# Queries in 512-byte rows with interleaved positions, loads by need, and a first block in two parts

## The chip, the cores and the metric

The kernel runs on one core of a Trainium2 chip. The metric is the device time of one execution in microseconds (us). A kernel's time is the median of its runs. A profile is taken of one of these runs, and its span is about 2 us shorter than the run's time (323.6 against 325.27 us for the kernel before).

The engines are PE (matrix products), DVE, ACT and POOL (elementwise work), and SP, whose queue issues nearly all loads and stores here. "SPq" and "ACTq" in a trace are the queues of SP and ACT when they issue a DMA. Where one of them waits, what stands behind it in the same queue waits too: in the changed kernel an activation on ACT starts at 73.45 us, 0.05 us after a transpose that ACT had been issuing since 71.93 left its queue.

## The reference

```
scores = q k^T / sqrt(64);  ret = scores * gamma_h^(i-j) for i >= j, else 0      # 8 batches, 8 heads, 576 tokens
x      = (ret v), heads side by side                                             # 4608 x 512
h      = x @ w_in;   g = h * sigmoid(beta * h);   out = g @ w_out                # 512 -> 2048 -> 512, float32 out
```

## The kernel before

Attention goes by tiles of 128 tokens. A tile needs its queries, keys and values scaled and cast to bf16, its queries and keys transposed, masked scores, values, a state product, and a cross product with the state of the earlier tiles. Its result is copied from PSUM into `xT`, the transposed input of the second part. That part goes by blocks of 512 tokens: "up" (x by w_in, then an activation on ACT into `gT`), then "down" (gT by w_out, copied to `ot` and stored). Block 8 is the "tail block": the last 64 tokens of each of the eight batches.

The order of the program is laid by hand. A list `fill` holds the steps of up and down. Streams of attention steps, each with a position, are merged into it. The parts that matter are these, with cuts marked `...`:

```python
def load(i):                                  # one tile: three loads of 256 KB, rows of 64 floats = 256 bytes
    t = stage.tile([P, 3, H, D], F32, name="qkvn", tag="qkvn", bufs=NQ)
    for j, src in enumerate((q, k, v)):
        ...
        nc.sync.dma_start(t[:, j], src[b, :, c * P:(c + 1) * P, :].rearrange("h s d -> s h d"))

def a_X(i):                                   # later tiles: transposed by a DMA that ACT issues
    nc.scalar.dma_start_transpose(qkT..., L["qk"]...)

def a_O(i):
    ...
    (nc.scalar.copy if i < CB else nc.vector.tensor_copy)(xT[:, :, x0:x0 + P], O[:])    # dense, bf16

def down(m, ms, f0, fn=4, n0=0, nn=d_model):
    ...
    nc.vector.tensor_copy(ot, po[:, :nn])
    if m < B:                                 # a batch's block: 128 rows in one store
        nc.sync.dma_start(out[r0:r0 + P, n0:n0 + nn], ot)
    else:                                     # the tail block, which comes last: two stores of 64 rows
        for x in range(2):
            nc.sync.dma_start(out[r0:r0 + TL, n0:n0 + nn], ot[x * TL:(x + 1) * TL])

for i in range(CB):                           # the first four tiles, with a filler matmul ahead of each
    warm_up(1, 256)
    a_sc(i); a_st(i); a_cross(i, True)
    ...                                       # cast of tile i + 1, or of weights
    a_O(i)
    ...                                       # transposes of tile i + 1
```

## Time and profile before

| | before |
|---|---|
| time, median of 3 | 324.23 us (323.68 to 324.70) |
| span of the profiled run | 323.6 us |
| first up matmul of block 0 | 20.71 us |
| first down of block 0 | 35.94 us |
| first up of block 1 | 56.62 us |
| first down of block 1 | 80.73 us |
| start of the last copy to `ot` | 318.09 us |
| from there to the end | 5.5 us |

The five points in time are the milestones. Each is read off PE's timeline (the first matmul of that kind), and the last one off DVE's. The prediction shows the stretches between them.

One more view of the kernel before is needed later: the copies into `xT`. The columns are the count, then the shortest, median and longest duration in ns, then when the first and last ran.

```profile
L280 DVE CAST xT<-O x32: 673/680/692, 50.0 to 262.8; 128x512 bf16<-128x512 f32 x32
L280 ACT CAST xT<-O x3: 586/586/586, 9.0 to 16.2; 128x512 bf16<-128x512 f32 x3
```

Every copy of one form takes the same time, 0.68 us on DVE and 0.59 us on ACT.

### The profile page before, as it was taken

Reading aid. Unit: us, or ns where it says so; the run is one execution under the profiler, and the core shown is the slowest. Engines: PE = TensorE matmul, PEld = TensorE weight load, DVE = VectorE, ACT = ScalarE, POOL = GpSimd, SP = SyncE. Lnnn points to the kernel's source line nnn. Section 1 sums busy time; section 2 is a strip of 40 time slices with the busy share of each in tenths; the row PEclk is TensorE's granted clock in tenths of the full one; section 3 lists DMA queues with packets and bytes.
Section 4 is the critical chain, followed back from the end, with each engine's and each line's share of the span. In section 5 each row is a group of like instructions: output and inputs, shape, how many; then the busy total and the mean of one; then the engine's idle time right before and its main releaser. Section 6 shows DMA issues by size and latency. Waiting matters only on the chain.

```text
span 323.6 us, 5348 instructions
## 1 busy us (share of the span) xinstructions
PE 303.9 (94%) x2122; PEld 156.0 (48%) x2157; DVE 114.3 (35%) x201; ACT 133.0 (41%) x242; POOL 105.2 (33%) x126
## 2 busy tenths in 40 slices
PE   7879987987999999999999999999999999999993
PEld 3543444865444544444444554444444544444452
DVE  6545666444243344323432353233323430020021
ACT  4547402675115721672047215730473047207500
POOL 4643773823556344431433336332430000000000
PEclk9999999999999999999999999999999999999999
DMA  9999999989999999999999999943213110011022
GB/s 169 218 361 388 353 197 218 198 217 184 188 235 218 186 249 191 217 249 169 242 240 209 182 226 193 207 94 98 67 39 61 65 67 0 32 65 35 0 65 67
DMA packets 152458, 53.85 MB, mean 166 GB/s; under 512 B 142944, under 2 KB 144368, under 8 KB 152432
## 3 DMA queue, kind: packets, MB, share of 16 engines
q1 hardware_dynamic: 122832, 46.15, 68.0%
q10 hardware_dynamic: 29600, 7.35, 15.9%
q8 instruction: 17, 0.28, 0.4%
q14 instruction: 9, 0.07, 0.1%
HBM read 36.71 MB, written 9.44 MB: 143 GB/s over the span
## 4 chain that ended last, share of the span: by engine, by line
PE 66%; DMA 15%; SPq 14%; issue 1%; POOL 1%; ACT 1%; DVE 1%; ACTq 0%; POOLq 0%
PE po L322 31%; PE ph L309 26%; SPq L84 13%; DMA qkvn<-in_v_dram 5%; DMA wt<-in_moe_w_in_dram 4%; DMA qkT<-qk 3%; PE O L270 2%; PE sc L237 2%; PE O L256 2%; DMA qkvn<-in_k_dram 2%; PE st L292 1%; SPq L148 1%; DVE w_in_sb L156 0%; ACTq L214 0%; SPq L81 0%
## 5 line engine op out<-in xcount | busy, mean ns | idle before, releaser
L309 PE MATMUL ph<-xT,w_in_sb 128*128 128x512 bf16 (+1 forms) x625 | 128.9, 357 | 4.1 <-POOL w_in_sb L156 1.3
L322 PE MATMUL po<-w_out_sb,gT 128*128 128x512 bf16 (+2 forms) x588 | 126.5, 367 | 1.9 <-ACT gT L311 0.9
L311 ACT ACTIVATE gT<-ph,beta_sb 128x512 bf16<-128x512 f32 (+1 forms) x160 | 100.3, 645 | 59.5 <-PE ph L309 53.4
L309 PEld LDWEIGHTS <-w_in_sb 128*128 128x128 bf16 x640 | 61.1, 98 | 63.5 <-POOL w_in_sb L156 1.9
L322 PEld LDWEIGHTS <-gT 128*128 128x128 bf16 x608 | 57.5, 98 | 63.7 <-issue 1.0
L242 DVE TENSOR_TENSOR R<-sc,causal 128x512 bf16<-128x512 f32 x72 | 46.3, 685 | 70.1 <-PE sc L237 70.1
L329 DVE COPY ot<-po 128x512 f32<-128x512 f32 (+2 forms) x38 | 25.1, 662 | 112.8 <-PE po L322 96.2
L202 POOL TENSOR_TENSOR qk<-qkvn,gq 128x512 bf16<-128x512 f32 x35 | 36.5, 1044 | 86.0 <-issue 29.4
L204 POOL TENSOR_TENSOR vn<-qkvn,gv 128x512 bf16<-128x512 f32 x36 | 37.8, 1049 | 27.2 <-DMA qkvn<-in_v_dram 14.0
L297 ACT CAST sbd<-st 64x256 bf16<-64x256 f32 x48 | 17.6, 366 | 59.3 <-PE st L292 48.7
L297 ACT CAST end<-st 64x256 bf16<-64x256 f32 x16 | 5.9, 367 | 42.2 <-PE st L292 40.8
L280 DVE CAST xT<-O 128x512 bf16<-128x512 f32 x32 | 21.8, 681 | 0.8 <-PE O L270 0.5
L203 POOL CAST qk<-qkvn 128x512 bf16<-128x512 f32 x28 | 17.4, 621 | 6.4 <-DMA qkvn<-in_k_dram 6.0
L270 PE MATMUL O<-R,vn 128*64 128x128 bf16 x288 | 16.2, 225 | 0.1
L237 PE MATMUL sc<-qkT 64*128 64x128 bf16 x288 | 14.3, 218 | 1.6 <-DMA qkT<-qk 0.8
L237 PEld LDWEIGHTS <-qkT 64*128 64x128 bf16 x288 | 8.2, 94 | 15.7 <-issue 11.7
L292 PE MATMUL st<-vn,qk 128*128 128x128 bf16 x128 | 12.4, 219 | 2.2 <-POOL vn L204 2.2
L270 PEld LDWEIGHTS <-vn 128*64 128x64 bf16 x288 | 10.0, 109 | 4.5 <-issue 0.7
L292 PEld LDWEIGHTS <-qk 128*128 128x128 bf16 x128 | 8.6, 97 | 3.6 <-issue 2.1
L168 POOL TENSOR_SCALAR w_out_sb<-wt,rbeta_sb 128x512 bf16<-128x512 f32 x4 | 8.5, 2113 | 3.7 <-DMA wt<-in_moe_w_out_dram 3.7
L256 PE MATMUL O<-qkT,sbd 128*128 128x128 bf16 x96 | 9.5, 221 | 0.0
L226 PE MATMUL T<-ident,qk 128*128 128x128 bf16 x64 | 6.0, 221 | 2.7 <-DVE xT L280 1.3
(46 smaller groups left out, 64.3 us busy)
## 6 DMA issues: line engine op xcount, KB each, us to landing
qkvn<-in_q_dram SPq DMA_DIRECT2D x32, 256.0 KB, 5.1
qkvn<-in_k_dram SPq DMA_DIRECT2D x32, 256.0 KB, 5.1
qkvn<-in_v_dram SPq DMA_DIRECT2D x32, 256.0 KB, 5.4
out_dram<-ot SPq DMA_DIRECT2D x32, 256.0 KB, 3.4
wt<-in_moe_w_out_dram SPq DMA_DIRECT2D x4, 1024.0 KB, 9.3
wt<-in_moe_w_in_dram SPq DMA_DIRECT2D x3, 1024.0 KB, 11.2
wt<-in_moe_w_in_dram SPq DMA_DIRECT2D x2, 512.0 KB, 6.9
qkvn<-in_q_dram SPq DMA_DIRECT2D x8, 128.0 KB, 4.8
```

The source lines that it names most:

```text
L84: nc.sync.dma_start(t[:, j], src[b, :, c * P:(c + 1) * P, :].rearrange("h s d -> s h d"))
L202: (nc.vector if i == 0 else nc.gpsimd).tensor_tensor(qk[:, 0], t[:, 0], gq_b, ALU.mult)
L204: nc.gpsimd.tensor_tensor(vn[:], t[:, 2], gv_b, ALU.mult)
L237: nc.tensor.matmul(sc[j][:, p, :], L["kT"][r, p, :], L["qT"][r, p, :], start=True, stop=True, skip_group_check=True)
L242: nc.vector.tensor_tensor(R[:, j], sc[j][:], m_b, ALU.mult)
L270: nc.tensor.matmul(O[j * D:(j + 1) * D, p, :], vn[:, 2 * p + j, :], R[:, j, p, :], start=p == 0 and not (early and crossed), stop=early or ...
L292: nc.tensor.matmul(st[:, p, :], heads(L["qk"][:, 1], p), heads(L["vn"], p), start=(c == 0 and p == 0), stop=True, skip_group_check=True)
L297: nc.scalar.copy(s[r, :, j * D:(j + 1) * D], st[r, :, j * D:(j + 1) * D])
L309: nc.tensor.matmul(ph[:, :tn], w_in_sb[:, ko, fo * P:(fo + 1) * P], xT[:, ko, x0:x0 + tn], start=(ko == 0), stop=(ko == KO - 1))
L311: nc.scalar.activation(gT[:, fo, t0:t0 + tn], ph[:, :tn], ACT.Silu, scale=beta_sb[:, fo:fo + 1])
L322: nc.tensor.matmul(po[:, :nn], gT[:, fo, ms * P:(ms + 1) * P], w_out_sb[:, fo, n0:n0 + nn], start=(fo == 0), stop=(fo == FO - 1))
L329: nc.vector.tensor_copy(ot, po[:, :nn])
```

## The change

The intent is to relieve the DMA at the start. A batch's queries come as rows in which four neighbouring positions lie side by side, so two loads with rows of 512 bytes stand where four loads read twice as many rows of 256 bytes. A partition then holds tokens 4p to 4p+3. Keys and values stay as they were, so the scores of a tile come out with interleaved columns: the mask is built for that order, and the copy into `xT` puts the columns back, with a step of four elements. Loads go out at chosen steps of the program. Block 0 starts when three of its four tiles are done, with parts of 384 and 128 tokens. The fillers between the first tiles are dropped. The tail block moves ahead of the last batch's block.

The diff, cut to its core:

```diff
+    blocks = list(range(B - 1)) + [B, B - 1]          # tail block before the last batch's
...
+    def load_q(b):
+        t = stage.tile([P, H, CB, D], F32, name="qn", tag="qn", bufs=2)
+        r = q[b, :, :MB, :].rearrange("h (p i) d -> p h (i d)", i=CB)
+        for u in range(2):
+            w = slice(u * CB * D // 2, (u + 1) * CB * D // 2)
+            nc.sync.dma_start(t.rearrange("p h i d -> p h (i d)")[:, :, w], r[:, :, w])
...
-    nc.gpsimd.affine_select(out=causal[:], in_=causal[:], pattern=[[1, P]], ...
+    nc.gpsimd.affine_select(out=causal[:], in_=causal[:], pattern=[[1, CB], [CB, PC]], ...
...
+        x = xt(B if b is None else b)[:, :, c * P:(c + 1) * P]
+        if b is not None:
+            x = x.rearrange("k p (s i) -> k p i s", i=CB)
+            O = O.rearrange("k p (i s) -> k p i s", i=CB)
-            (nc.scalar.copy if i < CB else nc.vector.tensor_copy)(xT[:, :, x0:x0 + P], O[:])
+            (nc.scalar.copy if i < CB else nc.vector.tensor_copy)(x, O[:])
...
-    for i in range(CB):
-        warm_up(1, 256)
+    for i in range(CB - 1):
         a_sc(i)
         a_st(i)
...
-    fill = [F(up, 0, fo) for fo in range(FO)]
+    fill = [F(up, 0, fo, 0, part) for fo in range(4)] + [F(up, 0, fo, part, MB - part) for fo in range(4)]
+    fill += [F(up, 0, fo) for fo in range(4, FO)]
...
+               [(12.2, F(load_q, 1))] + [(12.2, F(load_kv, n)) for n in range(CB, E)],
...
-            st += [(at, F(a_sc, i)), (at + 3, F(load, i + NQ))]
+                    st += [(at - 31, F(load_q, b)), (at - 19, F(pre_q, b, 0)), (at - 17, F(pre_q, b, 1)),
+                           (at - 13.5, F(x_q, b, 0)), (at - 12, F(x_q, b, 1))]
+                    st += [(at - 28, F(load_kv, n)), (at - 27.5, F(load_kv, n + 1)), (at - 15, F(pre, i)),
+                           (at - 14.5, F(pre, i + 1)), (at - 10.5, F(x_k, b, c // 2))]
```

## The prediction

> **What bounds the kernel now.** I read the page's busy shares first, then the table of stretches, then the start on PE, then the chain that ended last and the tail. The page:
>
> ```profile
> span 323.6 us, 5348 instructions
> PE 303.9 (94%) x2122; PEld 156.0 (48%) x2157; DVE 114.3 (35%) x201; ACT 133.0 (41%) x242; POOL 105.2 (33%) x126
> PEclk9999999999999999999999999999999999999999
> ```
>
> PE is busy for nearly the whole span at full clock; no other engine passes 41%. The stretches show where it is not (columns: stretch, length, then busy time of PE, PEld, DVE, ACT, POOL, clock, DMA share, GB/s):
>
> ```profile
> 0.00:20.70 20.70, 15.38 (x137) 8.86 (x137) 12.49 (x35) 10.52 (x22) 9.91 (x22) 1.00 1.15 226
> 20.70:35.94 15.24, 14.32 (x62) 6.16 (x65) 7.90 (x17) 10.29 (x15) 7.29 (x11) 1.00 1.05 387
> 44.00:56.62 12.62, 10.44 (x90) 5.65 (x93) 7.99 (x15) 2.64 (x6) 5.91 (x6) 1.00 1.36 222
> 56.62:80.73 24.11, 21.07 (x245) 16.88 (x244) 10.82 (x18) 15.68 (x39) 12.11 (x14) 1.00 1.08 199
> 80.73:318.40 237.67, 235.56 (x1557) 115.42 (x1587) 69.66 (x111) 93.14 (x160) 63.20 (x73) 1.00 0.76 141
> ```
>
> From 80.73 to 318.4 PE lacks 2 us of 238. Work there can be moved, not shortened: 25 matmuls of 512 columns take 5.39 us in the chain, 0.216 each, and one attention tile about 1.2 us (scores 0.33, values 0.34, state 0.22, cross 0.33). Time can be won in the first 80.73 us and in the last 5. In the first 20.7 PE holds only four tiles (5 us) and fillers; its waits:
>
> ```profile
> 18.48 0.38 PE L292 MATMUL st<-vn,qk 128*128 128x128 bf16 x4 [0.47 <-POOL vn L204]
> 20.71 0.39 PE L309 MATMUL ph<-xT,w_in_sb 128*128 128x512 bf16 x1 [0.95 <-POOL w_in_sb L156]
> ```
>
> A tile every 3.6 us: that is its three 256 KB loads at 218 GB/s, so the start is DMA-bound. And at the end of block 1 the chain runs over a late load, a POOL cast, a transpose issued by ACT, and only then the activation that PE wants:
>
> ```profile
> 71.86 6.25 DMA qkvn<-in_k_dram
> 78.16 0.62 POOL qk L203
> 78.80 1.35 ACTq L214
> 80.20 0.48 ACT gT L311
> 80.73 0.38 PE po L322
> ```
>
> ACT stands 3.2 us there. In block 1 it is full: 32 half activations of 0.44 (14.2), four state copies of 0.75 (3.0), two transposed-tile copies of 0.58 and four transpose issues of 1.25 to 1.87 (6.1) make 24.5, against a stretch of 24.1.
>
> **What the Trainium skill says.** (1) "DMA: Bandwidth & Descriptors", Specifications: line rate needs transfers of at least 512 B. The trace agrees for 256 B: 218 GB/s between 4 and 16 us (256-byte rows), 387 between 24 and 38 us (2 KB rows); 512-byte loads are not in it. (2) "SBUF — State Buffer", The DMA port swizzle: consecutive accesses inside a 16-byte line run at full rate. The new moving operand of scores and cross is runs of 32 bf16, 64 B, so I count no slowdown; the copies into xT now write every fourth bf16, 8 bytes apart, and this trace has nothing like it. (3) "TensorE: Matmul & The Clock Gate", What's actually happening: idle PE falls to half clock. The change drops the fillers between the first tiles; the clock was 1.00 in every stretch before, so this is a risk and no expectation.
>
> **The change, part by part.**
>
> *Queries in 512-byte rows.* A batch's 1 MB takes 4.8 us at 218 GB/s. At 387 it would take 2.7; halfway (a fixed cost per row, fitted to 256 B at 218 and 2 KB at 387, my estimate) 3.6. Gain 1.2 to 2.1 us of DMA per batch. After 80.73 it is hidden, PE being dense.
>
> *The start.* Loads begin to flow at about 3.0 (first landing 4.2 less 1.2). After: query halves land near 4.7 and 6.2, the first keys 7.4, then 1.2 each: values of tile 2 at 13.3. So DMA leaves the path, and a chain of engines takes its place, since keys are now transposed tile by tile behind the mask: key cast 0.43, transposes 0.35, copy 0.42, scores 0.40, mask 1.29, with 0.1 of signalling at each step: 3.4 per tile. The first has more ahead of it (POOL's query product ends 7.8, transposes 8.6, DVE's copy of twice the size 0.8, key transpose and copy): scores at about 10 in place of 6.8. Mask 0 ends 11.7, mask 1 15.1, mask 2 18.4; values and split copy follow, so block 0 begins at 19.7 in place of 20.71. This order leaves tile 3 (1.6 us with transposes) inside block 0.
>
> *Block 0 up.* Eight matmuls of 384 columns (1.3), key transpose and copy of tile 3 with a stall of 0.6, eight more (1.3), tile 3 to 24.8, its copy 0.6, sixteen of 128 columns (0.9) to 26.4. The third weight piece, which lands near 23 (before: 24.4), is ready. Then 48 matmuls, 10.4: up ends at 36.8 against 35.94. So here the change is 0.9 behind.
>
> *Block 0 down, tiles 4 and 5.* Before, 35.94 to 56.62: 20.7 us with over 3 us of idle PE, because tile 4's loads waited for w_out and POOL for its casts. After: the last w_out piece lands near 39 (before 40.76), is cast by 41.5, batch 1's queries land at 42 to 43, tile 4 by 45, tile 5 by 47.5. PE reaches the query transposes at 45.4, so it meets no wait. 16 steps of 0.863 (13.8), tile 4 (0.9), tile 5 (1.2), transposes (about 1.5), a mask wait 0.5 and the copy into xT at the end 0.8: 18.9. Block 1 starts at 55.7 against 56.62, 0.9 ahead.
>
> *Block 1 up.* ACT: 16 half activations (7.1) and 8 full (5.5), state copies of tiles 6 and 7 (1.5), four transpose issues (5 to 6.5), no transposed-tile copies: 19.1 to 20.6, plus about 1.9 of waits for tile 7 before the second half. Down of block 1 starts near 77.3. Before it started at 80.73 with tiles 8 and 9 and tile 10's scores done (2.45 of PE work), after with tile 8's scores only (0.33). Gain: 80.73 - 77.3 - 2.1 = 1.3, and about 0.3 more because loads now go out at fixed steps and not when a stage buffer comes free: 1.6.
>
> *From there.* The same matmuls, tiles and 28 DMA transposes; PE stays dense, so the lead of 1.6 is carried.
>
> *The tail.* The tail block now goes before the last batch's block, so the last rows leave with one transfer per piece in place of two:
>
> ```profile
> 318.09 0.29 DVE ot L329
> ```
> ```profile
> 320.06 1.19 SPq L336 DMA_DIRECT2D out_dram<-ot  x2
> ```
>
> Six issues of 0.6 queue behind each other until 321.25, though the last copy is done at 318.38. With three, each of the first two is issued before the next copy ends, and the last starts at 318.4 and ends at 319.0: gain 2.2.
>
> Sum: 1.6 + 2.2 = 3.8, so 324.2 - 3.8 = 320.4. I take 320.2.
>
> **The rivals.**
> 1. *The early loads win more.* If the start is worth what the DMA saves and the engine chain is shorter than I sum it (transposes and masks overlapping), block 0 begins at 17 to 18 and the lead grows to 4 or 5: 316 to 317. For: PE has over 20 us of slack before 80.73, and the author lays parts of 384 and 128 tokens for just this. Against: DVE must do cast, copy and mask in series for each tile.
> 2. *ACT as the bound.* ACT works in order, and a transpose that is not ready blocks the activations behind it, as at 78.80. In block 1 four transposes fall within some 11 steps, and the third and fourth wait for POOL, which has four query products of 1.04 and 1.65 for each tile in front. If the fourth waits 2 us, the gain of block 1 is gone and only the tail is left: 322.
> 3. *Strided access costs.* If a strided xT copy takes twice 0.68, up to 0.6 is added at each of four early copies on the path; if the 64-byte runs slow scores and cross by a quarter, 56 groups of 0.33 add 4.6. Together 323 to 327. Against: the 16-byte rule.
> 4. *DMA hidden anyway.* True from 80.73 on; the 10 us or so of DMA saved later are worth nothing.
>
> **Range and chances.** The tail is the surest term (1 to 2.5). The first 80 us may give -1.5 to +5. Hence 316.5 to 323.3. Over 2% faster needs less than 317.9, a gain of 6.3, which takes rival 1 nearly in full: 0.20. Slower by 2% needs rival 3 in full: 0.02. Within 2%: 0.78.
>
> **What would show it.** Step by step in the changed profile: 512-byte query loads at 290 to 390 GB/s in the first microseconds; first 384-column matmul at 19 to 20.5, with the mask chain ahead of it and no DMA; up of block 0 ending at 36 to 37.5; first half-width matmul of block 1 at 55 to 56.5; ACT full, not PE, until down of block 1 starts at 76 to 78.5; dense PE after it with scores still 0.33 for eight; three output issues after the last block's pieces and some 3 us from the last matmul to the end in place of 5.5. The prediction is wrong if the first block starts before 18 or after 21.5, if PE shows idle time after block 1, if the clock drops under 1.00 in the first block, or if scores or xT copies take longer than before.

## The result, and the profile after

The changed kernel takes **328.92 us** (median of 4 runs, 327.39 to 329.30) against 324.27 us for the kernel before on the same chip. The ratio is 1.0136, with a 95% interval of 1.0099 to 1.0173. Ratios here are the mean time of one kernel's fast runs over that of the other's fast runs of the same rounds, so they are not quite the ratio of the medians. Executions over 1.5% slower than the fastest of the same kernel are left out of the means. The result counts as the same at 2%, but the interval lies above 1, and the time is outside the predicted range.

One warning on the profiles: the profiled run of the kernel before was its slowest (325.27 us), and that of the changed kernel its fastest (327.39 us). The two spans therefore differ by 1.6 us where the medians differ by 4.65. Two more profiles of the unchanged changed kernel, taken later, are nearer the typical run, and so is the profile of an experiment (e4) that differs from the kernel before in the tail alone. Times are in us from the start of the span:

| | before | e4: before, new tail | after | after again (e13) |
|---|---|---|---|---|
| up of block 0 starts | 20.71 | 20.67 | 21.38 | 21.25 |
| down of block 0 starts | 35.94 | 35.91 | 41.12 | 41.63 |
| up of block 1 starts | 56.62 | 56.78 | 61.44 | 61.68 |
| down of block 1 starts | 80.73 | 80.28 | 83.17 | 84.88 |
| last copy starts | 318.09 | 317.36 | 322.48 | 324.53 |
| span | 323.6 | 320.2 | 325.2 | 327.2 |

The row of block 1's down needs a correction. The kernel before enters it with 2.45 us of attention on PE done (tiles 8 and 9 and the scores of 10), the changed one with 0.33 us. So 83.17 is really a lag of 83.17 - 80.73 + 2.12 = 4.6 us, and the last copy, 322.48 - 318.09 = 4.4 us late, agrees. The story is then short: 5.2 us are lost by the end of block 0's up, they are not won back in block 1, they are carried through the dense middle, and the tail returns 2.8.

The page of the changed kernel:

```profile
span 325.2 us, 5293 instructions
...
PE 306.7 (94%) x2137; PEld 156.5 (48%) x2137; DVE 132.9 (41%) x207; ACT 133.3 (41%) x232; POOL 101.7 (31%) x127
...
PEclk9559999999999999999999999999999999999999
```

DVE gained 18.6 us of work, and the second and third of the 40 slices show half clock, of which neither the clock row nor any duration of the kernel before shows a trace. The stretches between the milestones (columns as in the prediction: stretch, length, busy time of PE, PEld, DVE, ACT, POOL, clock, DMA share, GB/s):

```profile
0.00:21.38 21.38, 13.61 (x106) 9.04 (x107) 13.02 (x35) 8.91 (x16) 11.51 (x30) 0.69 1.09 246
21.38:41.12 19.74, 17.38 (x108) 8.99 (x108) 12.29 (x27) 13.70 (x23) 9.46 (x7) 0.90 1.04 365
41.12:61.44 20.32, 18.18 (x134) 9.56 (x133) 12.04 (x20) 3.19 (x7) 12.88 (x13) 1.00 1.09 244
61.44:83.17 21.73, 18.26 (x160) 11.95 (x160) 7.58 (x12) 12.89 (x27) 8.61 (x10) 1.00 0.98 214
83.17:322.50 239.33, 239.27 (x1633) 116.91 (x1631) 87.68 (x116) 94.61 (x162) 59.24 (x68) 1.00 0.65 132
```

The last line is as predicted: PE lacks 0.06 us of 239, so a lag at 83 us is a lag at the end. The second line is where most was lost: block 0's up takes 19.7 us in place of 15.2. PE's timeline shows how (start, length, instruction, count, and in brackets the idle time before it with what ended it):

```profile
14.37 0.61 PE L302 MATMUL sc<-qT,kT 64*128 64x128 bf16 x8
...
21.38 2.85 PE L381 MATMUL ph<-xT,w_in_sb 128*128 128x384 bf16 x8 [0.83 <-DVE rbeta_sb L443]
...
29.67 11.62 PE L381 MATMUL ph<-xT,w_in_sb 128*128 128x128 bf16 x64 [1.83 <-ACT xT L353]
```

Eight small matmuls take 0.61 where 0.40 is normal, and the first eight matmuls of 384 columns take 2.85; a few us later the same eight take 1.47. That is half clock. The last line is a wait of 1.83 us for ACT's copy of tile 3 into `xT`. The copies themselves:

```profile
L353 DVE CAST xT<-O x32: 679/1291/1310, 57.2 to 264.6; 128x512 bf16<-128x512 f32 x32
L353 ACT CAST xT<-O x3: 1301/1302/1307, 14.5 to 28.3; 128x512 bf16<-128x512 f32 x3
```

The median copy went from 0.68 to 1.29 us on DVE and from 0.59 to 1.30 on ACT. The shortest, 679 ns, are the tail's tiles, which are still written densely.

In block 1 the profile's chain of what released what, which in the kernel before went over one late load, goes over two here. This is its last part:

```profile
65.61 5.50 DMA qn<-in_q_dram
71.11 0.07 issue
71.18 2.05 POOL qs L234 x2
73.23 0.17 ACTq L262
73.45 0.48 ACT gT L383
73.97 0.61 PE ph L381 x4
```

Read from the bottom: PE waits for an activation, ACT's activation stands behind a transpose that ACT issues (L262), and the transpose waits for POOL's query products and these for a load of queries. The upper half must not be taken at its word. Releasers are inferred, and the load at 65.61 holds the queries of batch 3, whose products come after the transposes of batch 2 in the program. Batch 2's queries were issued at 49.24 and scaled at once. Then ACT's queue, with the two transposes of batch 2's queries and an activation between the second and the next one:

```profile
49.24 2.24 SPq L81 DMA_DIRECT2D qn<-in_q_dram  x2
...
55.47 4.04 POOL L234 TENSOR_TENSOR qs<-qn,gq 128x512 bf16<-128x512 f32 x4 [1.40 <-DMA qn<-in_q_dram]
...
70.47 1.33 ACTq L262 DMA_TRANSPOSE qT<-qs  x1
...
71.93 1.47 ACTq L262 DMA_TRANSPOSE qT<-qs  x1
73.45 0.47 ACT L383 ACTIVATE gT<-ph,beta_sb 128x256 bf16<-128x256 f32 x1 [1.12 <-POOL qs L234]
```

The query products were done at 59.5, 11 us before the first of these transposes. The key transposes follow at 73.58 and 78.70, with their casts done by 62.4 and 68.7, 11 and 10 us before. So batch 2's data were there. What PE waits for, 2.1 us in all, are activations that stand behind the transposes in ACT's queue, 1.25 to 1.47 us at each. I took this at first for late loads, held up by stores that wait in SP's queue for DVE. Such stores there are (at 51.57, 55.69 and 58.93), and they do delay loads, but nothing that PE waited for in this stretch waited for those loads.

And the tail:

```profile
322.48 0.29 DVE L401 COPY ot<-po 128x128 f32<-128x128 f32 x1 [0.60 <-PE po L394]
```

The last block's three stores, in place of six, are issued from 321.14 to 323.13, and the span ends 2.7 us after the last copy begins, in place of 5.5.

### The profile page after: what moved, and what is told of

Read it like the earlier page. It is cut to its first block, busy times and chain, and to the rows that moved or that the text cites. A ratio compares the mean times of both kernels' runs of the same rounds, so it can differ in the third digit from the quotient of the medians.

```text
span 325.2 us, 5293 instructions
## 1 busy us (share of the span) xinstructions
PE 306.7 (94%) x2137; PEld 156.5 (48%) x2137; DVE 132.9 (41%) x207; ACT 133.3 (41%) x232; POOL 101.7 (31%) x127
## 4 chain that ended last, share of the span: by engine, by line
PE 88%; DVE 3%; DMA 3%; POOL 2%; ACT 2%; SPq 1%; issue 1%; ACTq 0%; POOLq 0%; DVEq 0%
PE po L394 37%; PE ph L381 37%; PE O L339 4%; PE sc L302 3%; PE O L325 2%; PE st L365 2%; DMA qn<-in_q_dram 2%; DMA kvn<-in_v_dram 1%; PE ph L200 1%; DVE R L307 1%; POOL qs L234 1%; ACT xT L353 1%; SPq L91 1%; DVE kn L255 1%; SPq L404 1%
## 5 line engine op out<-in xcount | busy, mean ns | idle before, releaser
L381 PE MATMUL ph<-xT,w_in_sb 128*128 128x512 bf16 (+3 forms) x624 | 130.6, 365 | 7.6 <-DVE xT L353 2.8
L383 ACT ACTIVATE gT<-ph,beta_sb 128x512 bf16<-128x512 f32 (+3 forms) x156 | 100.5, 654 | 68.9 <-PE ph L381 64.5
L256 POOL TENSOR_TENSOR vn<-kvn,gv 128x512 bf16<-128x512 f32 x32 | 33.4, 1043 | 37.8 <-DMA kvn<-in_v_dram 14.5
L353 DVE CAST xT<-O 128x512 bf16<-128x512 f32 x32 | 38.9, 1216 | 3.0 <-PE O L339 2.2
L234 POOL TENSOR_TENSOR qs<-qn,gq 128x512 bf16<-128x512 f32 x27 | 28.0, 1060 | 37.5 <-DMA qn<-in_q_dram 37.4
L255 POOL CAST kn<-kvn 128x512 bf16<-128x512 f32 x24 | 14.6, 609 | 27.6 <-DMA kT<-kn 10.5
L302 PEld LDWEIGHTS <-kT 64*128 64x128 bf16 x288 | 8.5, 97 | 15.0 <-issue 11.4
L302 PE MATMUL sc<-qT,kT 64*128 64x128 bf16 x256 | 13.4, 227 | 1.4 <-DVE kT L285 1.4
L365 PE MATMUL st<-vn,kn 128*128 128x128 bf16 x128 | 13.1, 228 | 0.0
L325 PE MATMUL O<-qT,sbd 128*128 128x128 bf16 x96 | 9.9, 228 | 0.6 <-ACT xT L353 0.6
L365 PEld LDWEIGHTS <-kn 128*128 128x128 bf16 x128 | 8.7, 101 | 1.8 <-issue 0.6
```

The costliest lines, as they stand in the source:

```text
L234: e.tensor_tensor(batch[b]["qs"][:, i], q_tiles[b][:, :, i], gains(gq, i), ALU.mult)
L256: nc.gpsimd.tensor_tensor(vn[:], t[:, 1], gains(gv, c), ALU.mult)
L302: nc.tensor.matmul(view(sc[j][:, p, :]), L["kT"][r, p, :], rhs, start=True, stop=True, skip_group_check=True)
L353: (nc.scalar.copy if i < CB else nc.vector.tensor_copy)(x, O[:])
L365: nc.tensor.matmul(st[:, p, :], heads(L["kn"], p), heads(L["vn"], p), start=(c == 0 and p == 0), stop=True, skip_group_check=True)
L381: nc.tensor.matmul(ph[:, :tn], w_in_sb[:, ko, fo * P:(fo + 1) * P], xts[m][:, ko, t0:t0 + tn], start=(ko == 0), stop=(ko == KO - 1))
```

## The experiments

My theories at this point were: (A) the half clock, from the dropped fillers, costs the start; (B) the strided copies into `xT` cost 0.6 to 0.7 us wherever PE waits for one; (C) block 1 is paced by its own chain of late loads, POOL and ACT-issued transposes, so whatever the start wins or loses is swallowed there. (The late loads in C were my reading of the chain above; the trace doesn't bear them out.) The rivals were that the 512-byte rows or the split of block 0 do the harm, and for block 1 that ACT's queue alone or a collision of transfers is to blame. All kernels gave correct results. One table first, with the milestones from each profile, and times over 4 runs (e8: 5; e13 and e14: one run each, state unknown):

| kernel | up 0 | down 0 | up 1 | down 1 | span | median us | ratio to before (95%) |
|---|---|---|---|---|---|---|---|
| after | 21.38 | 41.12 | 61.44 | 83.17 | 325.2 | 328.92 | 1.0136 (1.0099 to 1.0173) |
| e1 fillers | 19.97 | 40.18 | 60.90 | 85.69 | 327.7 | 329.16 | 1.0149 (1.0098 to 1.0199) |
| e2 dense copies, permuted stores | 20.93 | 39.82 | 58.73 | 88.48 | 336.1 | 341.32 | 1.0510 (1.0467 to 1.0554) |
| e3 = e1 + e2 | 19.68 | 37.61 | 56.52 | 87.32 | 337.2 | 340.89 | 1.0494 (1.0453 to 1.0535) |
| e4 before, new tail | 20.67 | 35.91 | 56.78 | 80.28 | 320.2 | 321.87 | 0.9919 (0.9894 to 0.9944) |
| e5 near-dense copies | 20.87 | 38.31 | 57.67 | 83.69 | 325.8 | 330.32 | 1.0177 (1.0135 to 1.0218) |
| e6 = e5 + fillers | 20.66 | 38.11 | 57.02 | 84.85 | 327.3 | 328.40 | 1.0140 (1.0113 to 1.0166) |
| e7 256-byte query rows | 21.11 | 41.10 | 61.61 | 88.32 | 335.4 | 335.22 | 1.0359 (1.0296 to 1.0422) |
| e8 no 384/128 split | 25.03 | 41.26 | 61.90 | 87.42 | 329.4 | 329.55 | 1.0167 (1.0139 to 1.0195) |
| e9 early loads | 21.28 | 41.74 | 61.79 | 83.33 | 326.0 | 328.29 | 1.0140 (1.0101 to 1.0180) |
| e10 = e6 + e9 | 19.88 | 37.73 | 56.65 | 80.35 | 324.1 | 326.79 | 1.0057 (1.0012 to 1.0101) |
| e11 transposes from SP | 21.35 | 41.03 | 61.52 | 84.08 | 326.4 | 328.77 | 1.0139 (1.0106 to 1.0172) |
| e12 = e10 + e11 | 20.67 | 38.12 | 57.58 | 85.25 | 327.6 | 330.03 | 1.0179 (1.0148 to 1.0210) |
| e13, e14 after again | 21.25, 21.29 | 41.63, 41.65 | 61.68, 61.70 | 84.88, 84.97 | 327.2, 327.1 | 329.46, 329.35 | single runs |
| e15 = e10, later loads of batch 3 | 19.68 | 37.57 | 56.48 | 82.56 | 332.1 (slow) | 331.94 (2 of 4 slow) | 1.0138 (1.0081 to 1.0195) |
| e16 = e10, casts ahead of scores | 19.88 | 37.59 | 56.50 | 80.00 | 323.1 | 326.84 | 1.0106 (1.0080 to 1.0132) |

The kernel before had medians of 323.94 to 324.42 us beside these runs. Medians count all runs; e3 and e10 had one slow run of four each.

### e1: the fillers back

```diff
+    warm_up(1)
     t_q(0, 0)
     pre(0)
+    warm_up(1)
     t_q(0, 1)
 ...
     for i in range(CB - 1):
+        warm_up(1)
         a_sc(i)
         a_st(i)
+        warm_up(3 if i == 0 else 1)
```

> The changed kernel with filler matmuls put back between the first tiles. Theory A (the PE clock fell to half between 8 and 24 us because the fillers went): clock 1.00 in the first slices, the first eight 384-column matmuls take 1.3 us in place of 2.85, the first 512-column down matmul starts near 38 us in place of 41.1, and the time falls by 3 to 4 us, to about 325. Theory B (the strided copies into xT are the main loss): the copies still take 1.3 us each and hold the path, the time falls by less than 1.6 us (the stretched matmuls alone).

The matmuls of the first tiles are back at 0.40 us, and block 0 starts 1.4 us earlier:

```profile
17.00 0.40 PE L302 MATMUL sc<-qT,kT 64*128 64x128 bf16 x8
...
22.94 1.48 PE L381 MATMUL ph<-xT,w_in_sb 128*128 128x384 bf16 x8
...
27.04 1.47 PE L381 MATMUL ph<-xT,w_in_sb 128*128 128x128 bf16 x17 [1.82 <-ACT xT L353]
```

So theory A holds for the start. But the wait for ACT's copy stands, the clock falls after it (mean 0.57 between 28 and 32 us), and down of block 0 is only 0.9 us earlier. By block 1's down nothing is left, and the time is unchanged. The half clock is real, but it is not by itself what makes the kernel slower.

### e2 and e3: dense copies, the order undone in the store

```diff
-            x = x.rearrange("k p (s i) -> k p i s", i=CB)
-            O = O.rearrange("k p (i s) -> k p i s", i=CB)
...
-            nc.sync.dma_start(out[r0:r0 + P, n0:n0 + nn], ot)
+            nc.sync.dma_start(out[r0:r0 + P, n0:n0 + nn].rearrange("(s i) n -> i s n", i=CB), ot)
```

> The changed kernel with dense copies into xT: token columns stay interleaved inside a tile and the store puts the rows back in place. The result stays right. Theory B: every copy into xT is back at 0.68 us on DVE and 0.59 on ACT; on the path lie the split copy (0.3 to 0.7), that of tile 3 (0.7), 5 and 7 (0.6 each), so 2 to 3 us less, about 326. Theory A: clock still falls, block 0 still starts near 21, less than 1 us. Stores with rows four apart may land later but are hidden, except the last, under 0.5 us.

> Fillers and dense copies together. If A and B are both true and independent, the gains add: 5 to 7 us, about 322.5, under the kernel before. If they overlap (the same wait shortened twice), 4 us, about 325. A third theory C (ACT waits for the query products of batch 2, because the queries land late) keeps 2 us of idle PE in the second half of block 1 in all of these runs.

The copies are back at 0.68 and 0.59 us, and block 1 starts 2.7 us earlier than in the changed kernel, with fillers 4.9 us earlier, level with the kernel before (56.52 against 56.62). Theory B holds for the start. But the time is 12 us worse. The store with its four groups of rows is a new cost: the span ends 7.2 us after the last copy begins, against 2.7, and in block 1 the loads behind such stores come later and PE waits 8.2 us for `gT`, against 2.1. In block 1, ACT also issues two transposes that hold its queue for 5.3 and 4.0 us. The repair brought its own damage, so this pair says nothing on the total. A lead of 4.9 us at the start of block 1 was gone at its down, but with that damage in the same stretch it proves nothing for theory C.

### e4: the kernel before with the new tail only

```diff
+    blk = lambda b: B - 1 if b is None else B if b == B - 1 else b
-    col = [b * MB + c * P if b is not None else B * MB + c * P for b, c in seq]
+    col = [blk(b) * MB + c * P for b, c in seq]
...
-        if m < B:
-            r0 = m * S + ms * P
+        if m != B - 1:
+            r0 = min(m, B - 1) * S + ms * P
```

> The kernel before with only the order of the last two blocks changed: tail block ahead of the last batch's block, so that the last rows leave in one transfer per piece. Theory: the stretch from the last copy to the end shrinks from 5.2 to 2.4 us as in the changed kernel, and the time falls by 2.8, to 321.5. Rival: the new place of the tail block delays attention or stores and gives part of it back: 322.5 or more.

The tail alone is worth 324.42 - 321.87 = 2.5 us, and every milestone up to block 1 stays within 0.5 us. **This version is the fastest so far**, by 0.8% of the kernel before; that counts as the same at 2%, but the interval lies below 1. Its last two stores and last copy:

```profile
316.79 1.28 SPq L333 DMA_DIRECT2D out_dram<-ot  x2
...
317.36 0.29 DVE L330 COPY ot<-po 128x128 f32<-128x128 f32 x1 [0.60 <-PE po L323]
```

The prediction shows two of the six stores of the kernel before still being issued at 320.06, 2 us after its last copy began. Here the queue is empty 0.7 us after it. It also follows that the rest of the change costs 328.92 - 321.87 = 7 us, not 4.65.

### e5 and e6: copies in runs of 64 bytes, with the order kept dense

Here the columns of `xT` are ordered by remainder over the whole block, so that each copy writes runs of 32 elements and each store takes every fourth row:

```diff
-        x = xt(B if b is None else b)[:, :, c * P:(c + 1) * P]
+        x = xt(B if b is None else b)
...
-            x = x.rearrange("k p (s i) -> k p i s", i=CB)
+            x = x.rearrange("k p (i s) -> k p i s", i=CB)[:, :, :, c * PC:(c + 1) * PC]
...
+            rows = out[m * S:m * S + MB, n0:n0 + nn].rearrange("(p i) n -> p i n", i=CB)
+            nc.sync.dma_start(rows[:, ms], ot)
```

The partial up steps read and write with the same view. e6 adds the fillers of e1.

> The changed kernel with the token columns of a whole block ordered by their remainder by four, so that the copies into xT write runs of 32 bf16 and a store still takes 128 rows over all engines (rows four apart). The result stays right. Theory B (strided copies): copies at 0.68 on DVE and 0.59 on ACT, block 1 up starts near 58.7 us as in the run with permuted stores (61.4 in the changed kernel), and since the stores no longer hold up the loads this lead of 2.7 us is kept: about 326. Rival: the lead is lost in block 1, where ACT is full with transposes: 327.5 or more.

> The same with the fillers back. Theories A and B add: block 1 up starts near 56.5 us, down of block 1 near 78 in place of 83.2, clock 1.00 to there, about 323.5. Rival C (ACT is the bound in block 1): ACT still stalls PE there by 2 us or more, the clock drops after it, and the time stays at 326 or more.

The stores cost nothing this time (2.8 us from the last copy to the end), and the copies are at full speed:

```profile
L354 DVE CAST xT<-O x32: 678/680/692, 54.5 to 265.1; 128x512 bf16<-128x512 f32 x32
```

So the copies are repaired without a side effect at the end. Block 0's up takes 38.31 - 20.87 = 17.4 us in place of 19.7. Not all of this is theory B: 1.3 of the 2.3 us are the first eight matmuls of 384 columns, which took 1.54 us here in place of 2.85 though no filler was added, and 0.7 the shorter wait for ACT's copy (1.11 in place of 1.83). Block 1 starts 3.8 us earlier (e6: 4.4). The time does not move: 330.32 and 328.40. Block 1's up, 21.7 us in the changed kernel, now takes 26.0 and 27.8. ACT's timeline of e5 shows where the lead ends:

```profile
67.42 2.45 ACTq L262 DMA_TRANSPOSE qT<-qs  x1
...
70.05 3.21 ACTq L262 DMA_TRANSPOSE kT<-kn  x1
...
73.30 1.20 ACT L391 ACTIVATE gT<-ph,beta_sb 128x256 bf16<-128x256 f32 x3 [2.55 <-issue]
```

Two transposes, which in the first profile of the changed kernel hold ACT's queue for 1.47 and 1.25 us, hold it for 2.45 and 3.21, and the activations that PE needs stand behind them. PE's waits for `gT` grow from 2.1 to 4.9 us, and the clock halves after them. In e6 it is the same key transpose that holds longest:

```profile
69.75 4.04 ACTq L262 DMA_TRANSPOSE kT<-kn  x1
```

The four transposes of batch 2 hold ACT's queue for 8.2 us in e5 and 9.0 in e6, against 5.4 in the changed kernel. Late data are not the reason: in e5 the query products were done at 59.1 and the first keys' casts at 63.0, and their transposes were issued at 65.97, 67.42 and 70.05, about 7 us after.

### e7: the queries in 256-byte rows again

```diff
-        for u in range(2):
-            w = slice(u * CB * D // 2, (u + 1) * CB * D // 2)
+        for u in range(CB):
+            w = slice(u * D, (u + 1) * D)
```

> The changed kernel with queries loaded in 256-byte rows (four loads of 256 KB for a batch in place of two of 512 KB). If the 512-byte rows are worth what the rates say, the first query product starts as early, the first keys land 1.2 to 1.9 us later, and the time rises by 1 to 2 us. Rival: the loads are hidden behind the chain of key cast, transposes and mask: under 0.5 us.

Until block 1 nothing changes: 21.11, 41.10 and 61.61 against 21.38, 41.12 and 61.44. So the wide rows win nothing at the start, where the chain over engines, not the DMA, now sets the pace. After that 5 us are lost, and a wait on ACT shows it:

```profile
82.90 1.27 ACTq L262 DMA_TRANSPOSE kT<-kn  x1
84.22 1.84 ACT L383 ACTIVATE gT<-ph,beta_sb 128x512 bf16<-128x512 f32 x3 [4.93 <-issue]
```

In the changed kernel this transpose, for the second pair of batch 2's keys, is issued at 78.70. In e7 a load is late: SP sends for the keys of tile 10 only at 74.00, after 8.9 us of waiting for a query transpose of ACT's to land, and the second of this pair's casts starts at 82.26. Why four loads per batch in place of two end in this wait was not traced. So the wide rows are no cause of the loss; they save 335.22 - 328.92 = 6.3 us against narrow rows within this program. The experiment varies row size and number of loads together and doesn't part the two.

### e8: no split of block 0

Tile 3 is put back into the first loop, all sixteen up steps of block 0 are 512 wide, and the weights and loads take the positions of the kernel before.

```diff
-    for i in range(CB - 1):
+    for i in range(CB):
         a_sc(i)
...
-    fill = [F(up, 0, fo, 0, part) for fo in range(4)] + [F(up, 0, fo, part, MB - part) for fo in range(4)]
-    fill += [F(up, 0, fo) for fo in range(4, FO)]
+    fill = [F(up, 0, fo) for fo in range(FO)]
```

> The changed kernel without the parts of 384 and 128 tokens: tile 3 is done ahead of block 0, all 16 up groups are 512 wide, keys of tile 3 load ahead of the weights. If the split is worth what it is meant to be, down of block 0 starts 1 to 3 us later than 41.1 and the time rises as much. Rival: the split costs more than it gives (1.8 us of wait for the copy of tile 3, 0.5 for its keys, and it lets the clock fall), down of block 0 starts at 39 to 40 and the time falls by 1 to 2.

Block 0 starts 3.7 us later, and its down starts at 41.26 against 41.12. The split is worth 0.1 us there: the 3.7 us of early work are used up by the waits that tile 3 then has inside the block. It is neither the cause of the loss nor a gain.

### e9 and e10: the loads of batch 2 earlier, alone and with the other repairs

```diff
-               [(12.2, F(load_q, 1))] + [(12.2, F(load_kv, n)) for n in range(CB, E)],
+               [(12.2, F(load_q, 1))] + [(12.2, F(load_kv, n)) for n in range(CB, E)] +
+               [(12.2, F(load_q, 2))] + [(12.2, F(load_kv, n)) for n in range(E, E + 3)],
```

The loads that this puts into the queue ahead of the stores are taken out of their later steps. e10 is e5, the fillers and this together.

> The changed kernel with the loads of batch 2 (queries and the first three key and value tiles) issued right after those of batch 1, ahead of the first stores, and not at their fixed steps. Theory D (in block 1 the transposes that ACT issues come late because the loads of batch 2 sit in the sync engine's queue behind stores that wait for DVE): ACT's waits in block 1 go, idle PE there falls from 6.3 us to about 4 (the two copy waits), down of block 1 starts at 80 to 81 in place of 83.2, and the time falls by 2 to 4 us. Rival C (ACT's queue itself is full, 1.3 us for every transpose): idle PE stays within 0.5 us of 6.3, no change.

> Fillers, dense copies (columns by remainder) and early loads together. If A, B and D are all there is: up of block 1 starts at 57.0, down of block 1 near 78.5, clock 1.00 throughout, about 322. If C holds: down of block 1 not before 82, 326 or more.

Alone, against the two repeats of the changed kernel (e13, e14), the longest wait of PE for `gT` falls from 1.5 and 1.7 us to 0.8, the clock between 72 and 78 us stays at 1.00 in place of 0.72, and down of block 1 starts at 83.33 against 84.88 and 84.97. But the first profile of the changed kernel had a longest wait of 1.0 and 83.17 already, and the time, 328.29, is not to be told from 328.92. With the earlier start the edit counts: against e6, which lacks only this edit, down of block 1 comes at 80.35 in place of 84.85, and the time is 326.79 in place of 328.40.

What the edit does in SP's queue is not what its name says, though. Batch 2's queries go out no earlier (48.82 in e10, 49.60 in e9, 49.24 in the changed kernel); the keys and values of its first three tiles go out about 2 us earlier. The larger difference lies behind them: a load of SP's now waits 7.1 us (e9: 8.1) for a query transpose of ACT's to land, so the queries of batch 3 go out at 72.07 (e9: 74.12) in place of 65.7 in e6, and the loads of the tail after them. With that, the four transposes hold ACT's queue for 6.35 us in e10, against 9.0 in e6, and PE's waits for `gT` fall from 5.0 to 3.1. So the edit shows that the order of loads around these transposes is worth 4.5 us at the down of block 1. Since it moves loads of batch 2, of batch 3 and of the tail at once, it doesn't show which of them counts, and is no test of late data.

The three repairs together win 328.92 - 326.79 = 2.1 of the 7 us (by the fast runs alone, 1.0136 to 1.0057, about 2.6). Against e4, whose down of block 1 starts at the same time (80.28), e10's span is 3.9 us longer, all of it lost before block 2's up, which starts at 101.5 in place of 97.6. PE is busy 2.5 us longer in that stretch (19.65 against 17.16), with attention that e4 had done earlier, and 1.5 is a wait:

```profile
100.57 0.40 PE L302 MATMUL sc<-qT,kT 64*128 64x128 bf16 x8 [1.50 <-DMA kT<-kn]
```

### e11 and e12: the transposes issued by SP

```diff
-        nc.scalar.dma_start_transpose(dst...
+        nc.sync.dma_start_transpose(dst...
```

> The changed kernel with the transposes issued from the sync engine's queue in place of ACT's. Theory C: ACT's activations are no longer held, PE's waits for gT (2.1 us) and the clock drop after them go, down of block 1 starts 2 to 3 us earlier, the time falls by as much. Theory D: the transposed keys still come late, PE waits for them at the scores in place of gT, and the loads behind the transposes in that queue come later still: no change or slower.

> All four at once. If C and D each hold a part: down of block 1 at 77 to 78 and 320 to 321, under both kernels. If the sync engine's queue becomes the bound, later waits of PE for scores appear after block 1 and the time stays at 324 or more.

With the transposes off ACT, the activations no longer stand behind them. In e11 the middle of block 1's up runs through:

```profile
71.59 8.85 PE L381 MATMUL ph<-xT,w_in_sb 128*128 128x256 bf16 x56 [1.39 <-DVE xT L353]
```

The same 56 matmuls take 11.4 us in the changed kernel, from 69.77 to 81.18. So it is ACT's queue that held PE up there. But PE then waits for the transposed keys themselves, 1.6 us in e11 and, on top of the other repairs, far more in e12:

```profile
PE sc L302 <- DMA kT<-kn: 7.4, 1, 7.4
```

(That is the view of waits: total, times, longest.) The times are 328.77 and 330.03, so nothing is won. These keys were not late either: in e12 they were cast by 61.6 and their transpose was issued at 77.45, behind the loads of batch 3 and of the tail, which filled SP's queue from 65.34 on; in e11 it went out at 77.19, behind the loads of the tail. The edit moves the wait from one in-order queue to the other. A place in SP's queue ahead of those loads was not tried.

### e13 and e14: the changed kernel again

No edit; two more profiles.

> The changed kernel once more, one profile. If the half clock between 8 and 24 us is the rule, the mean clock is 0.974 again and down of block 0 starts near 41. If it is an accident (the mean clocks of the other runs were 0.995), the first slices show 1.00, down of block 0 starts at 38 to 39.5, and a stall with a clock drop after it stands in block 1 instead, so that the span is 326 to 327 all the same.

> The same kernel, a second profile, with the same two outcomes: either the early half clock and down of block 0 near 41, or a full early clock, an earlier block 0 and a stall in block 1.

The question was whether the half clock in the first profile was an accident of that run, since its mean clock was 0.974 and that of the other runs 0.995. In both new profiles the record shows full clock between 8 and 24 us, and yet the same matmuls take as long as before. From e13:

```profile
21.25 2.85 PE L381 MATMUL ph<-xT,w_in_sb 128*128 128x384 bf16 x8 [0.83 <-DVE rbeta_sb L443]
```

So slow matmuls at the start are the rule for this kernel, and the record of the clock can miss them. Durations, not the clock row, are to be read.

### e15 and e16: two more tries on e10

```diff
# e15
-                    st += [(at - 31, F(load_q, b))] if b > 2 else []
+                    st += [(at - (25 if b == 3 else 31), F(load_q, b))] if b > 2 else []
-                st += [(at - 27, F(load_tail, c)), ...
+                st += [(at - (21 if c == 0 else 27), F(load_tail, c)), ...
# e16, in the first loop
+        if i < CB - 2:
+            pre(i + 1)
+            t_k(i + 1)
         a_sc(i)
```

> The run with fillers, dense copies and early loads, with queries of batch 3 and the first tail tile loaded six steps later. Theory E (batch 2's transposes share the DMA engines with these loads): the second transpose takes 1.3 us in place of 2.5, PE's waits for gT in block 1 fall from 3.1 to under 2, down of block 1 at 79 or earlier in place of 80.4, time 1 to 2 us less than 326.8. Rival: they crawl for another reason, same times within 0.5; or the later loads hold up batch 3, and it is slower.

> The same run of all three repairs, with the key cast and transposes of the next tile put ahead of the mask of this one. If the start still counts: block 0 starts at 17.5 to 18.5 in place of 19.9, and 1 to 2 us come through to the end: 325. If block 1 sets the pace whatever the start does: block 1 up starts 1 to 2 us earlier, down of block 1 does not, and the time stays at 326 to 327.5.

e15 asked whether the loads of batch 3 and of the tail collide with the transposes of batch 2 and so stretch them. Two of its four runs, the profiled one among them, were slow; the ratio, 1.0138, shows no gain. It settles nothing: in e10, from which it starts, the queries of batch 3 went out after the first three transposes already (72.07), so there was little left to move. The collision is neither supported nor excluded. e16 asked whether the chain over DVE between the first tiles can be shortened by casting and transposing the next keys ahead of the scores. Block 0 starts at 19.88, as in e10, and the time is the same (326.84). It is no gain.

## Why the prediction was wrong

**The start, 19.7: measured 21.38.** The mechanism is right: no load is on the path, masks and keys follow each other. Scores run at 10.37, 14.37 and 17.91 where the text says "scores at about 10" and "3.4 per tile"; so 0.4 late at first, then 4.0 and 3.5 apart. The sum used durations at full clock. With fillers (e1) block 0 starts at 19.97, inside the 19 to 20.5 given as the test. The failed step is "the clock was 1.00 in every stretch before, so this is a risk and no expectation". A change that removes fillers from a stretch with 26% idle PE should have carried the slower case as an expectation. Two of the signs that the text gave for being wrong came true here: the clock fell under 1.00 in the first block, and the copies into `xT` took longer.

**Block 0 up, 17.1 us: measured 19.7.** Two terms were mis-sized. "Eight matmuls of 384 columns (1.3)" took 2.85 at half clock. And for tile 3 "its copy 0.6" was 1.30, with a wait of 1.83. With copies in 64-byte runs (e5) this stretch takes 17.4, where the first eight matmuls took 1.54 as well. Rival 3 had the size of the strided copy right, "up to 0.6 is added"; it measured 0.61 on DVE and 0.72 on ACT. The prediction kept it out of the sum "against: the 16-byte rule", though it had noted that nothing in the trace was like it.

**Block 0 down, 18.9: measured 20.3.** "The copy into xT at the end 0.8" became a wait of 1.4 us ahead of block 1, the same cause. The rest is not traced. The terms listed add up to 18.7, not 18.9.

**Block 1 up.** This is the step that decided. The text had 55.7 to 77.3, 21.6 us, and the trace has 21.73, so the length looks right, but by accident: it is the length at a start 5.7 us later than assumed. Where the start was nearer the assumed one (e5 and e6: 57.7 and 57.0), the stretch took 26.0 and 27.8 us; with the edit of e9 as well (e10: 56.65) it took 23.7. The failed step is the term "four transpose issues (5 to 6.5)", and with it the sum that takes ACT as full and never held up. The issues measured 5.4 us in the changed kernel, but 8.2 in e5 and 9.0 in e6 and 6.35 in e10, and PE waited for the activations behind them (2.1, 4.9, 5.0 and 3.1 us). The "about 0.3 more" from loads at fixed steps was not seen either. Rival 2 named the right queue ("ACT works in order, and a transpose that is not ready blocks the activations behind it"), but not the right reason: batch 2's products and casts were done 10 us and more before the transposes in the changed kernel, and about 7 us before the first three in e5. I had read such a wait in the kernel before, 78.16 to 80.73, where a late load is indeed behind it, and carried this reason over. (The text's count of ACT in that stretch, 24.5 of 24.1 us, is too high: its row of the table gives 15.68 us of work, and with 6.1 of issues that is 21.8.)

What stretches the issues stays open. In e5 and e6 they fall together with the loads of batch 3's queries and the first ones of the tail (from 65.7 and 66.0 on); in the changed kernel they come 4.5 us later, when those queries have landed, and in e10 those loads come later. So a collision with these loads is the likelier cause, but argued, not shown: the tail's loads run beside the transposes of the changed kernel too, and no run moves the loads of batch 3 alone.

**From there.** "PE stays dense, so the lead of 1.6 is carried" is right in its rule and wrong in its sign: a lag of 4.5 us was carried.

**The tail, 2.2: measured 2.5** (e4), by the mechanism given.

**512-byte rows.** "290 to 390 GB/s in the first microseconds" is right: they ran at 336 and 317 in the two slices from 3 to 5 us. That they are hidden later is right in the middle of the kernel. At the start they are worth nothing by themselves (e7).

The typical runs add up so: the span of the changed kernel (e13) is 7.0 us longer than e4's. At the down of block 0 the lag is 5.7 us. At the down of block 1 it is 84.88 - 80.28 + 2.1 = 6.7, at the last copy 7.2. The three repairs return 2.1 us of time. After them 4.5 to 5 of the 7 us are left.

Three things stay open. The first is what stretches the transposes: the second one of the queries holds ACT's queue for 2.45, 2.41 and 2.50 us in e5, e6 and e10, for 1.47, 1.93 and 2.14 in three profiles of the changed kernel and 1.27 in e9. Next, time minus span is 1.7 us for the kernel before and at least 2.2 for the changed one, so about 0.5 us of the 4.65 lies outside what the profile shows. And the wait of 1.5 us at 100.57 in e10 was not pursued.

## What to carry to other kernels

Before crediting a start with a gain, find the next place where an in-order queue sets the pace, and list what stands behind what in it: here activations stood behind DMA transposes, and the lead ended there. The chain in a profile is inferred. Before a load in it is called a cause, check in the program which tile it belongs to and when that tile's data were ready. A repair that moves one load moves those behind it too, so look at the whole queue afterwards. A reordered layout should be undone where it is free (here in stores of every fourth row, or in runs of 64 bytes), not in the engine's write, and a change of order should keep PE busy while it waits.

## What the Trainium skill lacked or had wrong

- "SBUF — State Buffer", The DMA port swizzle, says that one can stride for free within a 16-byte line, 8 bf16. Copies from PSUM with a step of 4 bf16 in the destination, two hits per line, took 1.29 in place of 0.68 us on DVE and 1.30 in place of 0.59 on ACT. Runs of 64 bytes took 0.68 and 0.59. As a rule for such writes it does not hold here. For PE's moving operand in runs of 64 bytes no slowdown was seen (eight scores 0.33 us).
- "TensorE: Matmul & The Clock Gate", What's actually happening, gives half clock as the default and after at least one idle window of about 3.4 us. From this row alone half clock would not be expected here: the longest wait among the first tiles was 1.72 us, and PE was busy 2.33 of 4 us between 8 and 12 us, at a clock of 0.53. The page says itself, under Seeing it yourself, that clock events in a trace have been seen to be unreliable on trn2; the runs agree, since eight matmuls of 384 columns took 2.85 us both where the record says 0.50 and where it says 1.00.
- "DMA: Bandwidth & Descriptors", Specifications, calls 512 bytes enough for line rate. Here 512-byte rows ran at 336 and 317 GB/s, weights in 2 KB rows at 386 from 20 to 28 us.
- No page that I read says, for trn2, how long a DMA transpose of this size holds the queue that issues it: 1.25 us at the least here, 3.21 in e5 and 4.04 in e6, with the activations behind it waiting.
